# Hashed attention and a gated MLP on one core: totals moved behind the next product, a narrower shift product, and two groups of transposes moved to VectorE

## Chip, cores and metric

The kernel runs on one core of a Trainium2 chip. The time is the device time of one execution, in microseconds (us). Of the kernel before there are three timed runs and one profiled execution, whose rows are quoted further down. The engines are called TensorE (PE in the rows; PEld is its loading of weights), VectorE (DVE), ScalarE (ACT), GpSimd (POOL) and SyncE (SP, which issues most DMAs).

## What is computed

Four batches, 8 heads of 64 dimensions, 768 positions. Each position is hashed to a bucket by the signs of six projections; a query sees the keys of its own bucket. The attention output, heads side by side, is the input x of a gated MLP with residual.

```python
q_bucket = sum(((q @ proj) > 0) * powers);  k_bucket = sum(((k @ proj) > 0) * powers)
scores = where(q_bucket == k_bucket, q @ k.T / sqrt(D), -1e9)
attn = exp(scores - max(scores));  attn = attn / (sum(attn) + 1e-09);  x = attn @ v
h = gelu(x @ w_in);  u, v = split(h)                      # 512 and 512 columns
v_n = (v - mean(v)) / sqrt(var(v) + 1e-6) * g_ln
out = x + (u * (w_sg @ v_n + b_sg)) @ w_out
```

## The kernel before

**Attention.** Two heads make a pair, so there are 16 pairs, and each pair is done in two half pairs of 384 queries: 32 half pairs. `parts` and `features` turn q and k by transposes (L500), split them into a high and a low part and compute the sign features (L520). For each block of 128 queries `largest` computes scores in rows (L540) and VectorE takes their maxima (L545, two of 952 ns a block, three blocks a half pair). `shift` takes the smaller of the maxima into a mostly zero tile m of 128 columns for each block (L552, VectorE), and three matmuls with m as weights (L558) turn that into a row of the features, so that `weigh` computes scores that are already shifted (L578, four products for each key block), ScalarE takes the exponential into p (L582) and GpSimd adds the p tiles up (L595). `weighted` is the product with v (L606): p has a 385th column of ones, so that the same product also gives the plain sum over v, which a query without a key in its bucket needs.

`finish` closes a half pair: four matmuls of a 32-column matrix of ones with the sums (`total`, L621) give the totals, ScalarE adds 1e-9 (tile sm) and copies the product out (un, L626), the totals go through DRAM to get them on many partitions for the reciprocal and back as rs, and five operations then make xt = un * rs + e, where e is the correction for queries without keys (three on ScalarE, one on VectorE, one on GpSimd). xt goes to DRAM as xs, the MLP's x transposed.

**MLP.** It is done per batch. `load_x` loads x and splits it (xh by ScalarE, xl by GpSimd, L707). `hidden_v` (L774) and `hidden_u` (L805) are the two halves of the first product with the gelu behind them, `gate` (L823) multiplies with w_sg, `project` (L849) with w_out, with three matmuls for each product of split numbers. `gate_weights` (L733 to L742) is done once: it loads w_sg in rows, TensorE transposes 36 blocks, ScalarE copies the high parts and VectorE subtracts for the low parts wgl. `project` adds the residual on TensorE too: for each of its 24 tiles of 128 positions, four transposing matmuls of x (tile rx, L854) into the same PSUM bank, then ScalarE copies the bank into ob, and a DMA stores it.

**What sets the order.** Every step is added to a `Plan` with an engine, an assumed cost and a priority. `order()` is a list scheduler: it simulates the engines, the DMA queues and the eight PSUM banks and emits the steps in the order that comes out. The priorities are made from the table at the top (`MLP`, `HID`, `AVP`, `S0P`, `PREP`, `SHIFTP`, `FINP`, `WSTEP`, `WP`). What runs is the fixed order for each engine with semaphores between them. Six of the eight banks, in pairs, are used by the scores of both kinds, and any free one by the rest. `form` in the plan is the shape of the weights ("row": 64 rows by 128 columns, "col": 128 by 64, "col32": 128 by 32).

Of the kernel before, what the change touches and what calls it, by code (L numbers as in the profile page):

```python
# [21 lines left out]
MLP = {"xl": "POOL", "gm": "DVE", "gl": "POOL", "wg": 463.45, "wo": -43.61, "x": 464.83}  # L22

BANKED = False
HID = 277.32
AVP = 3.21
S0P = 0.22
AHEAD = 4
PREP, SHIFTP, FINP, WSTEP, WP = 4.15, -4.68, 2.34, 48.11, -68.38
# [4 lines left out]
class Plan:  # L34
# [76 lines left out]
    def order(self):  # L111
# [32 lines left out]
        while len(out) < len(G):  # L144
# [26 lines left out]
            if e == "PE":  # L171

                work = g["c"] + (self.TURN_PE[g["form"]] if g["form"] != form else 0.0)
                form = g["form"]
# [62 lines left out]
def kernel(  # L237
# [32 lines left out]
    SCALE = 1.0 / math.sqrt(D)  # L270
    MISS = 2.0 ** 33
# [19 lines left out]
    less = const.tile([P, 1], F32, name="less")  # L291
    nc.vector.memset(less, -1.0)
# [36 lines left out]

    msts = [const.tile([P, HT, P], F32R, name=f"m{i}") for i in range(2)]  # L330
# [57 lines left out]
    xs = [[dram.tile([P, S], F32, name=f"xs_{b}_{hp}") for hp in range(NP)] for b in range(B)]  # L388
# [49 lines left out]
    if True:  # L438
# [23 lines left out]
        for i, t in enumerate(ptiles):  # L462
            (nc.vector if i % 2 else nc.gpsimd).memset(t[:, :, SH:SH + 1], 1.0)
# [65 lines left out]
        def largest(st, t, prio):  # L529

            hf, i = divmod(t, HT)
            if i == 0:
                st.mx = late.ring([P, 2, HT, 2], F32, "mx", 3)
# [9 lines left out]
            for kh in range(2):  # L543
                plan.add(PE, 0.346, prio + 0.01 * kh, lambda kh=kh: mm(kh), [*st.hi, *st.ft], [sc[kh]], form="row")
                plan.add(DVE, 0.95, prio, lambda kh=kh: nc.vector.tensor_reduce(  # L545
                    mx()[:, kh, i, :], sc[kh]()[:, :, :SH], axis=AX.X, op=ALU.max, negate=True), [sc[kh]], [(mx, (kh, i))])

        def shift(st, hf, prio):

            mx, m, tp = st.mx, plan.buf("m", len(msts), lambda i: msts[i % len(msts)]), ps_one()  # L550
            V = nc.vector
            plan.add(DVE, 0.16, prio, lambda: V.scalar_tensor_tensor(  # L552
                m()[:, :, MROW::BL], mx()[:, 0], EMPTY, mx()[:, 1], op0=ALU.min, op1=ALU.min),
                     [mx], [m], port=True)
# [5 lines left out]
            plan.add(PE, 0.33, prio, spread, [m], [tp])  # L560
# [5 lines left out]
        def weigh(st, hf, k0, prio):  # L566

            cs, kts = slice(hf * SH, (hf + 1) * SH), (k0, k0 + 1)
            if k0 == 0:
                st.sum, st.p = held.ring([P, 2, SH], F32, "sum", 2), []  # L570
# [27 lines left out]
        def weighted(st, prio):  # L598

            st.av, p = ps_one(), st.p  # L600
            av = st.av

            def product():
                for kt in range(NT):
                    for j in range(2):
                        nc.tensor.matmul(av()[row(j), :SH + 1], st.v()[:, j, kt, :], p[kt]()[:, j, :], start=(kt == 0), stop=(kt == NT - 1))  # L606
# [311 lines left out]
```

## Time and profile before

| | us |
|---|---|
| median of three runs | 790.71 |
| lowest and highest | 790.60, 790.88 |
| span of the profiled execution | 791.5 |

The profiled execution is thus 0.8 us longer than the median. In it TensorE is busy for 767.8 us. The attention takes about the first 475 us, at some 13.7 us for each half pair; the four MLPs follow, with hidden_v of batch 0 and its hidden_u ahead of the transposed gate weights. A matmul group in a timeline row has its start, how long it lasts (neighbours overlap, since matmuls are pipelined, so that the distance between two starts is the time one takes), the line and the tiles; x4 at the end of a row counts instructions.

### The profile page before, as it was taken

The numbers are of one execution on the slowest core, as the hardware profiler recorded it, in microseconds if no ns is written. First come the engines' busy times: TensorE is split into PE (matmuls) and PEld (weight loads), VectorE is DVE, ScalarE is ACT, GpSimd is POOL, SyncE is SP. The second block draws the span as 40 slices with busy tenths as digits, with TensorE's granted clock in tenths as the row PEclk, the third lists the DMA queues.
The fourth block names the chain that finished last, engine by engine and source line by source line (L and its number), as shares of the span: only waits on it lengthen the run. The fifth ranks groups of instructions, "written<-read, shape, count | busy, mean of one in ns | idle before, by whom it ended". The sixth has DMA issues, their size and how long they took to land.

```text
span 791.5 us, 14719 instructions
## 1 busy us (share of the span) xinstructions
PE 767.8 (97%) x5480; PEld 613.0 (77%) x5480; DVE 536.9 (68%) x862; ACT 421.1 (53%) x742; POOL 481.0 (61%) x522
## 2 busy tenths in 40 slices
PE   4999999999999999999999999799999999999998
PEld 3777776767677676767767669798898889988996
DVE  7978888989889888666766437868932167407630
ACT  2366576666656665655655566625632266116511
POOL 1478889898878778776867774665742235404230
PEclk9899999999999999999999999999999999999999
DMA  7032443245334414321320123400115311040003
GB/s 204 23 77 69 110 116 99 70 112 124 74 97 94 104 47 91 92 70 53 82 58 25 32 54 138 144 28 28 43 64 160 100 60 41 1 150 12 1 0 133
DMA packets 99304, 60.91 MB, mean 77 GB/s; under 512 B 64288, under 2 KB 91040, under 8 KB 99232
## 3 DMA queue, kind: packets, MB, share of 16 engines
q1 hardware_dynamic: 97920, 56.94, 26.5%
q10 hardware_dynamic: 1312, 3.02, 1.2%
q8 instruction: 43, 0.70, 0.4%
q14 instruction: 29, 0.24, 0.1%
HBM read 47.16 MB, written 12.78 MB: 76 GB/s over the span
## 4 chain that ended last, share of the span: by engine, by line
PE 86%; DVE 8%; DMA 2%; ACT 1%; issue 1%; POOL 0%; DVEq 0%; ACTq 0%; POOLq 0%; SPq 0%
PE psb L578 16%; PE psb L606 16%; PE psb L823 13%; PE psb L540 10%; PE psb L849 8%; PE psb L774 6%; PE psb L805 5%; PE psb L520 5%; PE psb L500 2%; DVE mx L545 2%; PE psb L621 2%; PE psb L558 2%; PE psb L854 1%; DVE m L552 1%; DMA sq<-s 1%
## 5 line engine op out<-in xcount | busy, mean ns | idle before, releaser
L595 POOL TENSOR_TENSOR sum<-sum,p 128x384 f32<-128x384 f32 x256 | 243.6, 983 | 8.4 <-ACT p L582 8.4
L545 DVE TENSOR_REDUCE mx<-psb 128x2 f32<-128x768 f32 x192 | 174.7, 952 | 63.1 <-PE psb L540 61.8
L582 ACT ACTIVATE p<-psb 128x768 f32<-128x768 f32 x192 | 145.7, 812 | 61.6 <-PE psb L578 60.2
L606 PE MATMUL psb<-p,v 128*64 128x385 f32 x768 | 131.2, 491 | 0.0
L606 PEld LDWEIGHTS psb<-p,v 128*64 128x64 f32 x768 | 52.3, 137 | 64.0 <-issue 62.8
L595 POOL TENSOR_TENSOR sum<-p,p 128x384 f32<-128x384 f32 x64 | 64.2, 1026 | 60.9 <-ACT p L582 60.9
L540 PE MATMUL psb<-fk,fq 64*128 64x384 f32 x384 | 72.6, 372 | 2.8 <-DVE mx L545 1.7
L759 DVE SCALAR_TENSOR_TENSOR h<-h,psb 128x384 f32<-128x384 f32 (+1 forms) x56 | 32.8, 606 | 58.5 <-ACT h L758 58.5
L834 POOL TENSOR_TENSOR gs<-gt,gs 128x384 fp32r<-128x384 f32 x32 | 33.2, 1041 | 59.2 <-ACT gs L831 59.2
L578 PE MATMUL psb<-hq,hk 64*128 64x384 f32 x384 | 68.8, 352 | 0.0
L540 PE MATMUL psb<-hk,hq 64*128 64x384 f32 x384 | 65.5, 335 | 0.0
L849 PE MATMUL psb<-woh,gs 128*128 128x512 f32 x192 | 65.4, 402 | 0.0
L578 PE MATMUL psb<-fq,fk 64*128 64x384 f32 x384 | 65.1, 332 | 0.0
L578 PE MATMUL psb<-lq,hk 64*128 64x384 f32 x384 | 65.0, 332 | 0.0
L578 PE MATMUL psb<-hq,lk 64*128 64x384 f32 x384 | 64.9, 332 | 0.0
L823 PE MATMUL psb<-wgh,zh 128*128 128x384 f32 x192 | 64.3, 335 | 0.0
L823 PE MATMUL psb<-wgh,zl 128*128 128x384 f32 x192 | 64.2, 334 | 0.0
L823 PE MATMUL psb<-wgl,zh 128*128 128x384 f32 x192 | 64.2, 334 | 0.0
L540 PEld LDWEIGHTS psb<-fk,fq 64*128 64x128 f32 x384 | 36.6, 185 | 30.2 <-issue 13.0
L826 DVE TENSOR_TENSOR gt<-psb,b_bc 128x384 f32<-128x384 f32 x32 | 17.8, 556 | 58.4 <-PE psb L823 34.9
L784 POOL TENSOR_TENSOR mv<-mv,epsr 128x1 f32<-128x1 f32 x24 | 14.1, 588 | 67.8 <-DVE mv L783 67.7
L626 ACT COPY un<-psb 128x385 f32<-128x385 f32 x32 | 15.5, 483 | 68.2 <-PE psb L606 68.2
(127 smaller groups left out, 1751.8 us busy)
## 6 DMA issues: line engine op xcount, KB each, us to landing
q<-in_q_dram SPq DMA_DIRECT2D x32, 192.0 KB
k<-in_k_dram SPq DMA_DIRECT2D x32, 192.0 KB
v<-in_v_dram SPq DMA_DIRECT2D x16, 384.0 KB
rs<-r SPq DMA_DIRECT2D x64, 96.0 KB
xs<-xt SPq DMA_DIRECT2D x32, 192.0 KB
x<-xs SPq DMA_DIRECT2D x16, 384.0 KB
rx<-xs SPq DMA_DIRECT2D x96, 64.0 KB
out_dram<-ob SPq DMA_DIRECT2D x24, 256.0 KB
```

Of the source, the lines that this page charges most:

```text
L520: nc.tensor.matmul(fp()[:, hf, :SH], w[:, s, :], x()[:, hf * SH:(hf + 1) * SH], start=(i == 0), stop=(i == 2))
L540: nc.tensor.matmul(sc[kh]()[:, j, :SH], x[0]()[row(j), qs], x[1]()[row(j), kh * SH:(kh + 1) * SH], start=(n == 0), stop=(n == 1))
L545: plan.add(DVE, 0.95, prio, lambda kh=kh: nc.vector.tensor_reduce(mx()[:, kh, i, :], sc[kh]()[:, :, :SH], axis=AX.X, op=ALU.max, negate=Tr ...
L578: nc.tensor.matmul(sc[i]()[:, j, :SH], x()[row(j), ks], y()[row(j), cs], start=(n == 0), stop=(n == 3))
L582: plan.add(ACT, 0.81, prio, lambda i=i: nc.scalar.activation(p[i]()[:, :, :SH], sc[i]()[:, :, :SH], AF.Exp), [sc[i]], [p[i]])
L595: plan.add(POOL, 1.03, prio + 0.6, lambda i=i, j=j, first=first: nc.gpsimd.tensor_add(sums()[:, j], (first or sums)()[:, j, :SH], p[i]()[: ...
L606: nc.tensor.matmul(av()[row(j), :SH + 1], st.v()[:, j, kt, :], p[kt]()[:, j, :], start=(kt == 0), stop=(kt == NT - 1))
L774: nc.tensor.matmul(ps(), x()[:, ts_], w[:, c, FH:FF], start=(c == 0 and n == 0), stop=(c == NC - 1 and n == 2))
L805: nc.tensor.matmul(ps()[:, :SH], w[:, c, fs], x()[:, cs], start=(c == 0 and n == 0), stop=(c == NC - 1 and n == 2))
L823: nc.tensor.matmul(vp()[:, :SH], z()[:, t, fs], w()[:, t, cs], start=(t == 0 and n == 0), stop=(t == NT - 1 and n == 2))
L834: nc.gpsimd if e == POOL else nc.vector).tensor_sub(gl()[:, cs], gt(), gh()[:, cs].bitcast(F32)),
L849: nc.tensor.matmul(po(), a()[:, ts_], w()[:, f, :], start=(f == 0 and n == 0), stop=False)
```

## The change

In the attention, `weighted` now issues the totals of the half pair before right behind the product with v, in one step; `last` does them for the final half pair. The ring of sums has three tiles instead of two, un has four. The 385th column of p is 1e-9/768 instead of one, so that one VectorE operation makes xt = (un + un's last column) * rs; the three ScalarE steps on e and vm and GpSimd's addition are gone. `shift` uses 66 instead of 128 columns of m as weights, and its minimum is a reduction over three values, one of them a constant.

In the MLP, w_sg comes by 24 DMAs of 768-byte runs into 32 x 32 blocks that lie so that VectorE's transpose (it turns blocks of 32 x 32) gives the wanted tile; ScalarE copies and GpSimd subtracts in tiles of 768 columns. rx of `project` comes in four DMAs a tile with 128-byte runs, VectorE transposes it into ob and later adds the bank to it; the four transposing matmuls and ScalarE's copy are gone. For the loads to reach over four pairs at once xs is one DRAM tile for each batch, and an rx load waits for all four pairs of its batch. The numbers in the planner's table change: those for the gate's weights, the output's weights and the load of x in `MLP`, and most of the others.

```diff
-MLP = {"xl": "POOL", "gm": "DVE", "gl": "POOL", "wg": 463.45, "wo": -43.61, "x": 464.83}
+MLP = {"xl": "POOL", "gm": "DVE", "gl": "POOL", "wg": 471.24, "wo": 97.53, "x": 447.95}
+NSUM = 3
-AVP = 3.21
-S0P = 0.22
+AVP = 0.98
+S0P = 2.0
...
-            (nc.vector if i % 2 else nc.gpsimd).memset(t[:, :, SH:SH + 1], 1.0)
+            (nc.vector if i % 2 else nc.gpsimd).memset(t[:, :, SH:SH + 1], 1e-9 / S)
...
-            plan.add(DVE, 0.16, prio, lambda: V.scalar_tensor_tensor(
-                m()[:, :, MROW::BL], mx()[:, 0], EMPTY, mx()[:, 1], op0=ALU.min, op1=ALU.min),
+            W = BL + 2
+            plan.add(DVE, 0.16, prio, lambda: nc.vector.tensor_reduce(
+                m()[:, :, MROW::BL], mx(), axis=AX.X, op=ALU.min), [mx], [m])
...
-                    nc.tensor.matmul(tp()[:, i * P:(i + 1) * P], m()[:, i, :], identr, start=True, stop=True)
+                    nc.tensor.matmul(tp()[:W, i * P:(i + 1) * P], m()[:, i, :W], identr, start=True, stop=True)
...
+                def both():
+                    product()
+                    total(sums, tp)
+                plan.add(PE, 1.3 * HT + 0.5, prio, both, p + [v_, sums], [av, tp], form=("col", "col32"))
...
-            plan.add(PE, 0.375, prio, total, [sums], [tp], form="col32")
...
-            plan.add(DVE, 0.56, prio, lambda: V.tensor_mul(xt(), un()[:, :SH], rs()), [un, rs], [xt], port=True)
-            plan.add(POOL, 0.98, prio, lambda: nc.gpsimd.tensor_add(xt(), xt(), e()), [xt, e], [xt])
+            plan.add(DVE, 0.56, prio, lambda: V.scalar_tensor_tensor(
+                xt(), un()[:, :SH], un()[:, SH:SH + 1], rs(), op0=ALU.add, op1=ALU.mult), [un, rs], [xt], port=True)
...
-                        nc.tensor.transpose(tp()[:, i * P:(i + 1) * P], wv[:, hf * HT + i, :], ident)
...
-                plan.add(PE, 0.36, prio + t, tr, [w], [tp])
-                plan.add(ACT, 0.37, prio + t, high, [tp], [(wgh, (t, hf))])
-                plan.add(DVE, 0.47, prio + t, low, [tp, (wgh, (t, hf))], [(wgl, (t, hf))])
...
+            plan.add(DVE, 0.96, prio + t, tr, [w], [wt])
+            plan.add(ACT, 0.84, prio + t, lambda wt=wt, ts_=ts_: nc.scalar.copy(wgh()[:, :, ts_], six(wt)), [wt], [(wgh, t)])
+            plan.add(POOL, 1.88, prio + t, lambda wt=wt, ts_=ts_: nc.gpsimd.tensor_sub(
...
+                    xs[b][:, t * P + g * Q:t * P + (g + 1) * Q].rearrange("(f b) a -> b f a", b=Q)), xd[b], [(rx, g)])
+            plan.add(DVE, 0.7, p0 - 5, lambda rx=rx, ob=ob: nc.vector.transpose(ob(), rx()), [rx], [ob])
...
-            plan.add(PE, 0.43, p0 + 0.1, residual, [rx], [po])
-            plan.add(ACT, 0.59, p0, lambda ob=ob, po=po: nc.scalar.copy(ob(), po()), [po], [ob])
+            plan.add(DVE, 0.7, p0, lambda ob=ob, po=po: nc.vector.tensor_add(ob(), po(), ob()), [po, ob], [ob])
```

In the order of instructions the change shows at three places. The first is TensorE in the attention, at the totals of a half pair; sum is the tile that GpSimd adds up, the rows above and below it are scores in rows (fk, fq the features, hk, hq and lq, lk the high and low parts) and the product with v. Before:

```order
L540 MATMUL psb<-fk_1_857,fq_1_839 128x384 x2
L540 MATMUL psb<-hk_1_686,hq_1_664 128x384 x2
L621 MATMUL psb<-sum_926,ones 32x192 x4
L578 MATMUL psb<-hq_1_664,hk_1_686 128x384 x2
L578 MATMUL psb<-hq_1_664,lk_1_700 128x384 x2
L578 MATMUL psb<-lq_1_692,hk_1_686 128x384 x2
L578 MATMUL psb<-fq_1_839,fk_1_857 128x384 x2
```

The same place on TensorE after the change (L610 is the product, L632 the totals, L544 and L581 the two kinds of scores):

```order
L610 MATMUL psb<-p_153,v_247 64x385 x2
L610 MATMUL psb<-p_154,v_247 64x385 x2
L632 MATMUL psb<-sum_728,ones 32x192 x4
L544 MATMUL psb<-fk_1_813,fq_1_792 128x384 x2
L544 MATMUL psb<-hk_1_663,hq_1_630 128x384 x2
L581 MATMUL psb<-hq_1_630,hk_1_663 128x384 x2
L581 MATMUL psb<-hq_1_630,lk_1_668 128x384 x2
L581 MATMUL psb<-lq_1_656,hk_1_663 128x384 x2
L581 MATMUL psb<-fq_1_792,fk_1_813 128x384 x2
```

The totals have moved from among the scores to the end of the product, where the weights already have few columns; and one block's row scores (L544, four matmuls) now stand between the groups of eight of L581, where before two blocks' stood together.

The second place is TensorE in the project of the last batch, where one tile of 128 positions ends and the next begins (woh and wol are w_out, gs the gated values). Before:

```order
L849 MATMUL psb<-woh_6049,gs_8480 128x512
L849 MATMUL psb<-wol_6070,gs_8480 128x512
L849 MATMUL psb<-woh_6049,gs_8488 128x512
L854 MATMUL psb<-ident,rx_8567 128x128 x4
L849 MATMUL psb<-woh_6049,gs_8339 128x512
L849 MATMUL psb<-wol_6070,gs_8339 128x512
L849 MATMUL psb<-woh_6049,gs_8344 128x512
```

And the same place after:

```order
L863 MATMUL psb<-woh_5868,gs_8190 128x512
L863 MATMUL psb<-wol_5885,gs_8190 128x512
L863 MATMUL psb<-woh_5868,gs_8198 128x512
L863 MATMUL psb<-woh_5868,gs_8049 128x512
L863 MATMUL psb<-wol_5885,gs_8049 128x512
L863 MATMUL psb<-woh_5868,gs_8054 128x512
```

The transposing matmuls are gone and nothing stands in their place: one tile's products follow the other's.

The third place is TensorE behind hidden_u of batch 0 (xh and xl are the split x, wih and wil the first weights, the gs rows w_sg before its transposes). Before:

```order
L805 MATMUL psb<-xh_2181,wih 128x384
L805 MATMUL psb<-xl_2273,wih 128x384
L805 MATMUL psb<-xh_2181,wil 128x384
L733 MATMUL psb<-ident,gs_5714 128x128 x6
L733 MATMUL psb<-ident,gs_5718 128x128 x6
L733 MATMUL psb<-ident,gs_5726 128x128 x6
L733 MATMUL psb<-ident,gs_5732 128x128 x6
L733 MATMUL psb<-ident,gs_5747 128x128 x6
L733 MATMUL psb<-ident,gs_5763 128x128 x6
L774 MATMUL psb<-wih,xh_5957 128x512
L774 MATMUL psb<-wil,xh_5957 128x512
L774 MATMUL psb<-wih,xl_5967 128x512
```

And after (L816 is hidden_u, L785 hidden_v of the next batch):

```order
L816 MATMUL psb<-xh_2221,wih 128x384
L816 MATMUL psb<-xl_2340,wih 128x384
L816 MATMUL psb<-xh_2221,wil 128x384
L785 MATMUL psb<-wih,xh_5764 128x512
L785 MATMUL psb<-wil,xh_5764 128x512
L785 MATMUL psb<-wih,xl_5773 128x512
```

The 36 transposes are gone, and the next batch's hidden_v, which needs that batch's split x, follows directly. Over the whole stretch 57 matmuls of that hidden_v stand ahead of the gate of batch 0, where before there were 15.

## Rows read from the trace of the kernel before

**Rows 1.** The page: busy time of each engine; then the chain's shares by engine.

```profile
PE 767.8 (97%) x5480; PEld 613.0 (77%) x5480; DVE 536.9 (68%) x862; ACT 421.1 (53%) x742; POOL 481.0 (61%) x522
...
PE 86%; DVE 8%; DMA 2%; ACT 1%; issue 1%; POOL 0%; DVEq 0%; ACTq 0%; POOLq 0%; SPq 0%
```

**Rows 2.** Windows: stretch, us, PE, PEld, DVE, ACT, POOL busy, clock, DMA share, GB/s.

```profile
30.00:120.00 90.00, 90.00 (x791) 65.72 (x789) 77.60 (x103) 57.71 (x96) 74.04 (x78) 1.00 0.31 82
690.00:712.00 22.00, 22.00 (x111) 18.23 (x110) 1.12 (x2) 4.04 (x7) 1.55 (x2) 1.00 0.40 129
```

**Rows 3.** TensorE's timeline at one half pair's totals: start, duration, instructions.

```profile
94.48 0.44 PE L540 MATMUL psb<-fk,fq 64*128 64x384 f32 x2
94.76 0.34 PE L540 MATMUL psb<-hk,hq 64*128 64x384 f32 x2
94.93 0.34 PE L540 MATMUL psb<-fk,fq 64*128 64x384 f32 x2
...
97.12 0.45 PE L540 MATMUL psb<-fk,fq 64*128 64x384 f32 x2
97.41 0.34 PE L540 MATMUL psb<-hk,hq 64*128 64x384 f32 x2
97.67 0.53 PE L621 MATMUL psb<-sum,ones 128*32 128x192 f32 x8
98.14 0.45 PE L578 MATMUL psb<-hq,hk 64*128 64x384 f32 x2
98.42 0.34 PE L578 MATMUL psb<-hq,lk 64*128 64x384 f32 x2
```

**Rows 4.** The same view at the shift's product (L558).

```profile
88.59 0.34 PE L520 MATMUL psb<-lq,pwh 128*128 128x384 f32 x1
88.84 0.55 PE L558 MATMUL psb<-identr,m 128*128 128x128 f32 x3
89.23 0.40 PE L520 MATMUL psb<-hk,pwh 128*128 128x384 f32 x1
89.47 0.34 PE L520 MATMUL psb<-hk,pwl 128*128 128x384 f32 x1
```

**Rows 5.** Groups by shape: busy us, mean ns, idle before and what ended it.

```profile
L558 PEld LDWEIGHTS psb<-identr,m 128*128 128x128 f32 x96 | 13.5, 193 | 8.4 <-DVE m L552 7.2 <-ACT p L582 0.7 <-issue 0.3
L500 PEld LDWEIGHTS psb<-ident,q 128*128 128x128 f32 x96 | 10.7, 146 | 6.9 <-issue 4.2 <-DVE wy L374 2.7
L545 DVE TENSOR_REDUCE mx<-psb 128x2 f32<-128x768 f32 x192 | 174.7, 952 | 63.1 <-PE psb L540 61.8 <-ACT h L758 0.6
L826 DVE TENSOR_TENSOR gt<-psb,b_bc 128x384 f32<-128x384 f32 x32 | 17.8, 556 | 58.4 <-PE psb L823 34.9 <-POOL gs L834 23.5
L707 POOL TENSOR_TENSOR xl<-x,xh 128x768 fp32r<-128x768 f32 x16 | 29.8, 1870 | 3.2 <-ACT xh L709 3.2
```

**Rows 6.** The chain of waits in the last project: start, duration, engine and line.

```profile
768.59 2.77 PE psb L849 x12
771.35 0.44 PE psb L854 x4
771.79 2.78 PE psb L849 x12
```

**Rows 7.** TensorE's timeline around the gate's transposes; in brackets a wait and its releaser.

```profile
496.10 3.17 PE L733 MATMUL psb<-ident,gs 128*128 128x128 f32 x21
...
504.31 0.47 PE L774 MATMUL psb<-wih,xh 128*128 128x512 f32 x1
...
507.62 0.50 PE L774 MATMUL psb<-wih,xh 128*128 128x512 f32 x1 [1.67 <-DVE wgl L742]
...
509.82 0.34 PE L823 MATMUL psb<-wgh,zh 128*128 128x384 f32 x1
```

**Rows 8.** Windows: transfers in 256-byte pieces; hidden_u of batch 1. Columns as Rows 2.

```profile
380.00:386.00 6.00, 6.00 (x47) 3.45 (x46) 3.42 (x6) 2.98 (x8) 4.59 (x5) 1.00 0.89 178
540.00:570.00 30.00, 28.16 (x140) 26.24 (x139) 27.54 (x68) 18.54 (x38) 18.98 (x28) 0.94 0.08 23
```

More of the change, by code (lines that the diff above doesn't have):

```diff
@@ L328 @@
     nc.vector.memset(fv[:, 3, :, MROW:MROW + 1], 1.0)
+    mxs = [const.tile([P, HT, 2, 3], F32, name=f"mx{i}") for i in range(3)]
+    for t in mxs:
+        nc.vector.memset(t[:, :, :, 2:3], EMPTY)
     msts = [const.tile([P, HT, P], F32R, name=f"m{i}") for i in range(2)]
@@ L387 @@
     PE, DVE, ACT, POOL, SP = "PE", "DVE", "ACT", "POOL", "SP"
-    xs = [[dram.tile([P, S], F32, name=f"xs_{b}_{hp}") for hp in range(NP)] for b in range(B)]
+    xs = [dram.tile([DM, S], F32, name=f"xs_{b}") for b in range(B)]
     plan = Plan()
@@ L605, in product @@
                     for j in range(2):
[L606 to L613 removed]
+                        nc.tensor.matmul(av()[row(j), :SH + 1], v_()[:, j, kt, :], p[kt]()[:, j, :], start=(kt == 0), stop=(kt == NT - 1))
@@ new lines, in weighted @@
+            if owed is None:
+                plan.add(PE, 1.3 * HT, prio, product, p + [v_], [av], form="col")
+            else:
+                sums, tp = owed.sum, ps_one()
+                def both():
+                    product()
+                    total(sums, tp)
+                plan.add(PE, 1.3 * HT + 0.5, prio, both, p + [v_, sums], [av, tp], form=("col", "col32"))
+            half.un = un = late.ring([P, SH + 1], F32, "un", 4)
+            plan.add(ACT, 0.48, prio - 1, lambda: nc.scalar.copy(un(), av()[:, :SH + 1]), [av], [un])
@@ new lines, in weighted, with total, last @@
+            if owed is not None:
+                finish(owed, tp, prio)
+            return half
+        def total(sums, tp):
+            for j in range(2):
+                for a in range(2):
+                    r = 64 * j + 32 * a
+                    nc.tensor.matmul(tp()[r:r + 32, :QH2], ones, sums()[:, j, a * QH2:(a + 1) * QH2], start=True, stop=True)
+        def last(half, prio):
+            sums, tp = half.sum, ps_one()
+            plan.add(PE, 0.375, prio, lambda: total(sums, tp), [sums], [tp], form="col32")
+            finish(half, tp, prio)
@@ L614, in finish @@
+        def finish(st, tp, prio):
+            hf, un = st.hf, st.un
+            sm = late.ring([P, QH2], F32, "sm", 3)
             sq, rs, xt = late.ring([P, W6], F32, "sq", 3), late.ring([P, SH], F32, "rs", 3), late.ring([P, SH], F32, "xt", 2)
             V = nc.vector
-            def total():
-                for j in range(2):
-                    for a in range(2):
-                        r = 64 * j + 32 * a
-                        nc.tensor.matmul(tp()[r:r + 32, :QH2], ones, sums()[:, j, a * QH2:(a + 1) * QH2], start=True, stop=True)
@@ L680 @@
                 if c % HT == HT - 1:
[L681 to L682 removed]
+                    owed = weighted(sts[n], hf, 2 * g + AVP, owed)
+        last(owed, 2 * g + FINP)
     M_ = MLP
```

86 lines of the change are left out of this document (34 added, 52 removed).

## The prediction

> **What bounds the kernel now.** The page comes first: TensorE is busy for 767.8 of 791.5 us, and 86% of the chain of waits is TensorE's [rows 1]. The windows tell where that is a hard bound. In 90 us of the attention and in 22 us of the last project TensorE is busy without a gap at a granted clock of 1.00, which is the 2.4 GHz level [rows 2]. There a us taken from TensorE is a us of the end, until another engine is full. VectorE is the nearest: 77.60 of 90 us, 11.8 us of a half pair of 13.7; GpSimd has 74.04. In the project VectorE has 1.12 of 22 us. So prices are read as distances between starts in TensorE's timeline, and each one asks whether VectorE or GpSimd can follow.
>
> **Totals.** Two plain pairs of score matmuls start 0.17 us apart (94.76 to 94.93) [rows 3]. Around the totals the distances are 0.26 (97.41 to 97.67), 0.47 (to 98.14) and 0.28 (to 98.42), in all 1.01 us for three steps of which two are plain pairs, 0.34. The totals cost 0.67, of which about 0.20 is the change into another shape of weights and back. Behind the product the weights already have few columns, and the change back to the scores is paid by the product anyway, as at 94.48 to 94.76 (0.28). What remains is the 0.47 of the totals themselves, or 0.36 if the 0.11 that a first pair pays goes as well. So 0.20 to 0.31 is saved, 31 times (the last total stands alone): 6.2 to 9.6 us. I take **6.2**, since going from 64 to 32 columns is a change of shape too, and every change in the rows costs something. If it costs 0.10 more than that, 3.1 stay. The sums are those of the half pair before, finished some 13 us earlier, so the product waits for nothing new. Three ScalarE operations and GpSimd's 0.98 us go from each half pair; neither engine bounds here, so I count nothing for them. The one VectorE operation that replaces a multiplication of the same tile is also counted at nothing; if it went at half speed, VectorE would have 0.56 us more in 13.7, which its idle 1.9 hide.
>
> **Spread.** From 88.59 to 89.47 TensorE takes 0.88 us for three matmuls with m and two plain ones [rows 4]. The part from 88.84 to 89.23 is 0.39; less the 0.11 of a first pair, 0.28 remain, 0.093 for each. The columns that move through (128) don't change, only those of the weights, 128 to 66. If the weights' load sets the step, 62/128 of 0.28 goes, 0.13 a half pair, 4.2 us for 32; from the whole 0.39 it would be 0.19, 6.0 us. If the moving columns set it, nothing. I take **4.2**, because the load of these weights takes 193 ns [rows 5], longer than the step, so that it can't be hidden by one neighbour. A loss is bounded by the difference of two loads of 128 columns, 193 against 146 ns: 0.05 a half pair, -1.6 us.
>
> These loads are of fp32r; loads of 128 fp32 columns (L500) take 146 ns, less than the 193, so no row shows the fp32r load as the fast one [rows 5]. The Trainium skill, "TensorE: Matmul & The Clock Gate", section "Weight-path perf modes — Fast Weight Load (FWL) and DoubleRow", says that a fast load is on when there are exactly 128 weights and the type isn't FP32, measured at about twice the speed; 66 columns would then lose it. The rival for it is below.
>
> **Residual on VectorE.** In the last project a tile with its four transposing matmuls takes 3.20 us (768.59 to 771.79), of which 0.44 lie between 771.35 and 771.79 [rows 6]. 24 tiles: **10.6** us. The cover must hold: VectorE gets a transpose and an addition of 512 columns in each tile. An addition from PSUM of 384 columns takes 556 ns [rows 5], so 741 ns for 512, 1.5 us for both, in 2.77 us of TensorE and on an engine that is nearly idle there. A 32 x 32 transpose isn't in the trace; at twice an addition both take 2.2, still covered. The loads: a tile is 262 KB, before in pieces of 512 bytes, now of 128. A window with 256-byte pieces moves 178 GB/s at a share of 0.89, so 200 at full share [rows 8]. Half the piece at half the rate is an estimate of 100 GB/s, 2.6 us for a tile. That is close to 2.77, but the gate's 144 matmuls stand ahead of the project: two tiles can be loaded and turned into ob, and two more loaded, before the project starts, and only two of six remain. SP issues as many DMAs as before. If the cover fails, the rival on loads has the price.
>
> **Gate weights on VectorE.** The block of transposes lasts from 496.10 to 504.31, 8.2 us, and at 507.62 TensorE waits another 1.67 us for the last low part before the gate can start at 509.82 [rows 7]. Both go: 9.9 us. But the block also covered the split of the next batch's x. Its tiles are free only when the last hidden_u of batch 0 is through, and now the next hidden_v stands right there. The first low part needs 1.87 us on GpSimd [rows 5] behind ScalarE's copy, so at least 2 us are exposed; with all four parts one after the other 7.5 us. The new order takes one part of x with several tiles of positions in a row, which hides the later parts; I take 3.4 exposed, **6.5** net, and keep 2 to 8 (10 if the split is done ahead).
>
> **What the new numbers of the planner do.** Two places. In the row scores, one step goes from 97.12 to 97.41, 0.29 where a plain one takes 0.17, with the longer first row of an engine that had stopped [rows 3]. Here TensorE had caught up with the engines that empty the banks. One or two such stops in each half pair are 3.8 to 7.7 us in all. In the new order four matmuls of row scores alternate with eight of the shifted ones, so the two engines that empty banks take turns; half of the stops should go: **3**, with 6 either way, since the new alternation can stop elsewhere. And in hidden_u of batch 1, from 540 to 570, TensorE is busy for 28.16 of 30 us at a mean clock of 0.94 [rows 8]: 1.8 us idle and 1.8 by the clock, which falls behind a stop. The new order may heal it or make another: **0**, 4 either way.
>
> **Sum.** 6.2 + 4.2 + 10.6 + 6.5 + 3 + 0 = 30.5 us of 791.5: a span of 761.0. The profiled execution was 0.8 longer than the median of the runs, which gives **760** us.
>
> **Rivals.**
> - *The narrow weights and the order bring nothing* (moving columns set the step, the stops stay): 760 + 4.2 + 3 = 767. For it: the number of columns that move is unchanged, and which engine stops TensorE isn't settled. Against it: the 193 ns.
> - *The fast load is lost* with 66 columns. At half the speed a load of 66 columns lasts 193 x 2 x 66/128 = 199 ns, as long as before: the 4.2 go, 764. Against it stand the 146 ns of a type that would never be fast.
> - *GpSimd makes the MLP wait.* It now has the low parts of the gate weights (six of about 1.87 us, 11.2) beside those of x (7.5), 18.7 us together. If they come one after the other behind hidden_u, the 57 matmuls of hidden_v that stand ahead of the gate, 13 us at the 0.23 that one of 512 columns takes [rows 6], don't cover them: 5.6 us of wait, and the 6.5 of the gate weights are lost: 772. Against it: w_sg doesn't depend on x and can be done during hidden_u.
> - *Loads set the project.* A tile would have to take 10 us (26 GB/s): the fifth, whose load can start some 6 us in, when its buffer is free, would land at 16 and the sixth at 26, where TensorE ends at 16.6, so 9.4 us at the end of the last batch; in the other batches TensorE goes on: 769. Against it: 100 GB/s is what the rows make likely. The Trainium skill, "DMA: Bandwidth & Descriptors", section "Specifications", puts the smallest transfer for full rate at 512 bytes, so 128-byte runs are below it; by that rule alone the loads get slower, as in the estimate, and only the size of it decides.
> - *The alternation makes VectorE the bound of the row scores, slower than before.* Four row matmuls and eight shifted ones last 2 x 0.17 + 4 x 0.17 = 1.04 us, and VectorE's maximum for them 0.952 [rows 5]. Only 0.09 is left for its other work in that stretch. If each of six alternations in a half pair came 0.17 late, 192 x 0.17 = 33 us would be lost, 793; that is the point from which the change is slower. For it: VectorE has 11.8 - 6 x 0.95 = 6.1 us of other work in each half pair. Against it: that work can lie beside the product (4 us) and the features, and 14% of VectorE's time is idle.
> - *Nothing changes*, since what TensorE no longer does was a wait for others: 790. The windows without a gap speak against it.
>
> **Chances.** My forecast 0.60, narrow weights and order without effect 0.18, fast load lost 0.04, GpSimd 0.08, loads 0.04, VectorE bound 0.04, nothing 0.02. The range is **750 to 772**: the terms' own bounds go to 3.1, -1.6, 2, -3 and -4 on the bad side and 9.6, 6.0, 8, 9 and 4 on the good side; they won't all fall on one side, and some 10 to 12 us either way remain. Faster by over 0.2% (about what a measurement of this kernel can tell from no change): 0.94; within 0.2%: 0.02; slower: 0.04.
>
> **What would show it.** Right: in the trace of after the product is followed by the totals 0.4 to 0.5 us before the next scores, with no totals among the scores; the shift's three matmuls take some 0.26 instead of 0.39; the tiles of the projects follow each other at 2.77 us; hidden_v of batch 1 starts within 2 to 4 us behind hidden_u of batch 0; VectorE's idle time in the attention is above 10%. Wrong: TensorE's rows of scores with waits on VectorE's maxima in each alternation; a wait ahead of the gate on GpSimd's low parts; project tiles that wait for ob or for rx; a half pair that isn't at 13.3 us, which is 13.7 less 0.20, 0.13 and 0.1.

## The result

The kernel after takes 758.14 us (median of four runs, 757.51 to 758.49), before on the same chip 790.8. The ratio is 0.9574 with a 95% interval of 0.9558 to 0.959: 4.3% faster, some 33 us. The forecast was 760, in a range of 750 to 772. The time agrees; the terms of the sum don't all agree, and the errors cancel. That is what the experiments are about. Their effects are given as differences of such ratios times 790.8, since each group of runs had its own runs of the kernel before beside it.

The page of the kernel after, busy times and the chain by engine, to be held against [rows 1]:

```profile
PE 731.8 (97%) x5348; PEld 594.0 (79%) x5348; DVE 563.8 (75%) x906; ACT 376.0 (50%) x616; POOL 464.4 (61%) x496
...
PE 84%; DVE 7%; DMA 6%; issue 1%; ACT 1%; SPq 0%; ACTq 0%; DVEq 0%
```

TensorE has 36.0 us less work and is still busy for 97%: it still bounds the kernel. Windows of the kernel after (columns as [rows 2]): the attention, and the stretch behind hidden_u of batch 0:

```profile
30.00:120.00 90.00, 89.17 (x807) 66.49 (x805) 78.53 (x104) 53.10 (x82) 72.94 (x75) 1.00 0.34 84
...
475.00:490.00 15.00, 11.58 (x32) 7.99 (x33) 12.50 (x19) 8.92 (x16) 10.84 (x10) 0.66 0.82 157
```

The attention runs at full clock with VectorE idle for 13%, and one half pair follows the other at 13.13 us instead of 13.78 (mean distance between the starts of two products with v). The second row is new: TensorE busy for 11.58 of 15 us at a mean clock of 0.66.

Where the time went is read best by adding, for each line, the distances from each matmul's start to the next one's start, over the whole trace. A wait thus counts for the line that ran before it. A second trace of the kernel before (the run before_again below) serves as the base, since it is the more ordinary one:

| TensorE's time, start to start, us | before | after | difference |
|---|---|---|---|
| scores, both kinds (L540 + L578; L544 + L581) | 223.9 | 213.5 | -10.4 |
| totals (L621; L632) | 14.8 | 14.8 | 0.0 |
| shift's product (L558; L561) | 13.0 | 8.3 | -4.8 |
| turning q and k, features (L500 + L520; L504 + L524) | 70.4 | 63.8 | -6.6 |
| project and residual (L849 + L854; L863) | 76.8 | 66.8 | -10.0 |
| gate's transposes (L733) | 8.1 | none | -8.1 |
| hidden_v (L774; L785) | 71.4 | 77.2 | +5.8 |
| hidden_u (L805; L816) | 69.6 | 71.1 | +1.5 |
| product with v, gate, start | 234.1 | 234.4 | +0.3 |
| sum | 782.1 | 749.8 | -32.3 |

### The profile page after: what moved, and what is told of

It reads as the page before. It is cut to its first block, busy times and chain, and to the rows that moved or that the text cites. A ratio compares the mean times of both kernels' runs of the same rounds, so it can differ in the third digit from the quotient of the medians.

```text
span 755.7 us, 14344 instructions
## 1 busy us (share of the span) xinstructions
PE 731.8 (97%) x5348; PEld 594.0 (79%) x5348; DVE 563.8 (75%) x906; ACT 376.0 (50%) x616; POOL 464.4 (61%) x496
## 4 chain that ended last, share of the span: by engine, by line
PE 84%; DVE 7%; DMA 6%; issue 1%; ACT 1%; SPq 0%; ACTq 0%; DVEq 0%
PE psb L581 17%; PE psb L610 15%; PE psb L834 11%; PE psb L863 9%; PE psb L544 9%; PE psb L785 7%; PE psb L816 7%; PE psb L524 4%; PE psb L504 3%; PE psb L632 2%; DMA x<-xs 2%; DMA gs<-in_moe_w_sg_dram 1%; DMA ow<-in_moe_w_out_dram 1%; DVE mx L549 1%; PE psb L561 1%
## 5 line engine op out<-in xcount | busy, mean ns | idle before, releaser
L598 POOL TENSOR_TENSOR sum<-sum,p 128x384 f32<-128x384 f32 x256 | 247.8, 1004 | 0.0
L549 DVE TENSOR_REDUCE mx<-psb 128x2 f32<-128x768 f32 x192 | 181.5, 956 | 50.2 <-PE psb L544 41.8
L585 ACT ACTIVATE p<-psb 128x768 f32<-128x768 f32 x192 | 155.5, 815 | 62.0 <-PE psb L581 58.4
L610 PE MATMUL psb<-p,v 128*64 128x385 f32 x768 | 131.2, 491 | 0.0
L610 PEld LDWEIGHTS psb<-p,v 128*64 128x64 f32 x768 | 52.3, 137 | 63.2 <-issue 60.8
L544 PE MATMUL psb<-fk,fq 64*128 64x384 f32 x384 | 68.3, 352 | 2.2 <-DVE fk L527 1.2
L581 PE MATMUL psb<-hq,hk 64*128 64x384 f32 x384 | 65.4, 337 | 2.0 <-DVE mx L549 1.2
L581 PE MATMUL psb<-fq,fk 64*128 64x384 f32 x384 | 64.4, 332 | 0.0
L544 PE MATMUL psb<-hk,hq 64*128 64x384 f32 x384 | 64.4, 332 | 0.0
L581 PE MATMUL psb<-lq,hk 64*128 64x384 f32 x384 | 64.3, 331 | 0.0
L581 PE MATMUL psb<-hq,lk 64*128 64x384 f32 x384 | 64.3, 331 | 0.0
L863 PE MATMUL psb<-woh,gs 128*128 128x512 f32 x192 | 60.4, 391 | 0.8 <-DVE ob L866 0.8
L769 ACT ACTIVATE h<-psb 128x384 f32<-128x384 f32 (+1 forms) x56 | 29.6, 535 | 55.7 <-PE psb L785 42.0
L801 POOL TENSOR_TENSOR zl<-y,zh 128x512 fp32r<-128x512 f32 x24 | 32.7, 1361 | 29.6 <-ACT zh L800 29.5
L544 PEld LDWEIGHTS psb<-fk,fq 64*128 64x128 f32 x384 | 35.9, 184 | 13.4 <-issue 6.4
```

Of the source, the lines that this page charges most:

```text
L544: nc.tensor.matmul(sc[kh]()[:, j, :SH], x[0]()[row(j), qs], x[1]()[row(j), kh * SH:(kh + 1) * SH], start=(n == 0), stop=(n == 1))
L581: nc.tensor.matmul(sc[i]()[:, j, :SH], x()[row(j), ks], y()[row(j), cs], start=(n == 0), stop=(n == 3))
L585: plan.add(ACT, 0.81, prio, lambda i=i: nc.scalar.activation(p[i]()[:, :, :SH], sc[i]()[:, :, :SH], AF.Exp), [sc[i]], [p[i]])
L598: plan.add(POOL, 1.03, prio + 0.6, lambda i=i, j=j, first=first: nc.gpsimd.tensor_add(sums()[:, j], (first or sums)()[:, j, :SH], p[i]()[: ...
L610: nc.tensor.matmul(av()[row(j), :SH + 1], v_()[:, j, kt, :], p[kt]()[:, j, :], start=(kt == 0), stop=(kt == NT - 1))
L863: nc.tensor.matmul(po(), a()[:, ts_], w()[:, f, :], start=(f == 0 and n == 0), stop=(f == NF - 1 and n == 2))
```

## The experiments

**Totals apart.** The totals are a step of their own again, among the scores.

```diff
-                    owed = weighted(sts[n], hf, 2 * g + AVP, owed)
-        last(owed, 2 * g + FINP)
+                    last(weighted(sts[n], hf, 2 * g + AVP, None), 2 * g + 2.34)
```

> The kernel after, with the totals of each half pair as a step of their own among the score matmuls, not behind the product; three of the four planner costs and all else stay. Theory (each change of the weights' shape costs TensorE about 0.1 us on the way in and out): +0.20 us a half pair, +6.2 us for 31, so about 764. Rival (the place of the totals is worth nothing, what was gained is GpSimd's and ScalarE's lighter work and the order of the scores): 758, as the kernel after.

Measured: 771.87 us, ratio 0.9742 (0.9723 to 0.9761), +13.3 us against the kernel after, twice the theory's number. TensorE's timeline of this run at one of the totals, start and duration first:

```profile
91.90 0.34 PE L581 MATMUL psb<-fq,fk 64*128 64x384 f32 x2
92.71 0.53 PE L632 MATMUL psb<-sum,ones 128*32 128x192 f32 x8 [0.47 <-DVE mx L549]
93.17 0.44 PE L544 MATMUL psb<-fk,fq 64*128 64x384 f32 x2
93.45 0.34 PE L544 MATMUL psb<-hk,hq 64*128 64x384 f32 x2
```

The steps are 0.81, 0.46 and 0.28 us. The usual distance into the totals is 0.27 (median of the 32 half pairs; the 0.81 here has a wait in it), and 0.27 + 0.28 less two plain 0.17 is 0.20: the price of the two changes of shape, as forecast. In the same sums as above (the profiled execution of this run took 773.37) the scores take 9.6 us more, the two hidden products 5.8. So 6.2 is the shape, and the rest is stops and a different order in the MLP, which this edit moves as well. The rival, that the place is worth nothing, is out.

**Width of the shift's product.**

```diff
-            W = BL + 2
+            W = P
```

> The kernel after, with 128 instead of 66 weight columns in the shift's product and nothing else changed, the order of all instructions included. Theory (the load of the weights sets the step; in the traces 0.112 us a matmul at 128 columns and 0.060 at 66): 3 x 0.052 x 32 = +5.0 us, about 763. Rival 1 (the moving columns set it, and what shrank around this product was a wait for VectorE): 758. Rival 2 (a fast load that only 128 columns get): faster than the kernel after, below 758.

Measured: 762.79 us, ratio 0.9626 (0.9608 to 0.9644), +4.1 us. TensorE's timeline at this product, first with 66 columns (kernel after), then with 128 (this run):

```profile
108.93 0.34 PE L524 MATMUL psb<-lq,pwh 128*128 128x384 f32 x1
109.11 0.34 PE L561 MATMUL psb<-identr,m 128*66 128x128 f32 x3
109.29 0.39 PE L524 MATMUL psb<-hk,pwh 128*128 128x384 f32 x1
```

```profile
110.07 0.34 PE L524 MATMUL psb<-lq,pwh 128*128 128x384 f32 x1
110.25 0.45 PE L561 MATMUL psb<-identr,m 128*128 128x128 f32 x3
110.53 0.39 PE L524 MATMUL psb<-hk,pwh 128*128 128x384 f32 x1
```

Three matmuls take 0.18 us against 0.28, and their weights' load 137 ns (mean after) against 193 [rows 5]. The number of weight columns sets the step, as the columns that move through are the same. The rival with moving columns is out, and so is the one with a fast load for 128 columns: 66 are faster by more than a third, with no sign that 128 had an advantage to lose.

**Residual on TensorE.**

```diff
-            plan.add(DVE, 0.7, p0 - 5, lambda rx=rx, ob=ob: nc.vector.transpose(ob(), rx()), [rx], [ob])
-            plan.add(DVE, 0.7, p0, lambda ob=ob, po=po: nc.vector.tensor_add(ob(), po(), ob()), [po, ob], [ob])
+            plan.add(PE, 0.43, p0 + 0.1, residual, [rx], [po])
+            plan.add(ACT, 0.59, p0, lambda ob=ob, po=po: nc.scalar.copy(ob(), po()), [po], [ob])
```

> The kernel after, with the residual added on TensorE as before (four transposing matmuls a tile, ScalarE's copy), loads of rx in 512-byte runs. Theory (TensorE bounds the projects): +0.42 us a tile, +10 us for 24, about 768. Rival (VectorE's additions and the 128-byte loads cost part of it back): +5 or less, 763.

Measured: 770.9 us, ratio 0.9727 (0.9713 to 0.9742), +12.1 us. The chain of the last project in this run has the same two rows as [rows 6], at the same durations:

```profile
746.14 2.77 PE psb L860 x12
748.91 0.44 PE psb L865 x4
749.35 2.78 PE psb L860 x12
```

Ten to eleven of the twelve us are these matmuls, the rest is order in the MLP. Nothing of the gain was given back on VectorE or by the loads. In the kernel after, the groups of VectorE's transposes and additions (busy, mean ns, idle before) are these:

```profile
L859 DVE STREAM_TRANSPOSE ob<-rx 128x512 f32<-128x512 f32 x24 | 16.8, 704 | 5.7 <-DMA out_dram<-ob 4.5 <-DVE y L797 0.8 <-DMA rx<-xs 0.3
L866 DVE TENSOR_TENSOR ob<-psb,ob 128x512 f32<-128x512 f32 x24 | 16.3, 685 | 19.4 <-PE psb L863 19.1
```

Both were estimated at 741 ns. The 128-byte loads are waited for 0.3 us in all, and TensorE's project waits once for ob, 0.8 us.

**Gate weights on TensorE.** The loop of the kernel before is put back whole; its core:

```diff
-            plan.add(DVE, 0.96, prio + t, tr, [w], [wt])
+                plan.add(PE, 0.36, prio + t, tr, [w], [tp])
```

> The kernel after, with the gate weights transposed on TensorE as before (36 transposes, 12 ScalarE copies, 12 VectorE subtractions). The prediction had 6.5 us for this edit. Theory after seeing the trace (VectorE is full from 455 to 490 us, its transposes of 1.65 us delay the gelu, and TensorE then waits 4.8 us behind hidden_u and runs at the low clock for some us): only about 3 us, so 761. Rival 1 (the prediction's step): 764 to 765. Rival 2 (it was a loss, the waits cost more than the transposes did): 756.

Measured: 756.42 us, ratio 0.9545 (0.953 to 0.956), 2.3 us *faster* than the kernel after; the two intervals just touch. The part of the change that was to bring 6.5 us brings nothing, and probably costs some 2. TensorE's timeline behind hidden_u, first of the kernel after, then of this run:

```profile
473.26 0.34 PE L816 MATMUL psb<-xh,wil 128*128 128x384 f32 x1
475.71 0.59 PE L785 MATMUL psb<-wih,xh 128*128 128x512 f32 x1 [2.11 <-ACT xh L726]
476.11 0.63 PE L785 MATMUL psb<-wil,xh 128*128 128x512 f32 x1
477.62 0.80 PE L785 MATMUL psb<-wih,xl 128*128 128x512 f32 x1 [0.88 <-POOL xl L724]
478.21 0.63 PE L785 MATMUL psb<-wih,xh 128*128 128x512 f32 x1
```

```profile
473.97 2.15 PE L750 MATMUL psb<-ident,gs 128*128 128x128 f32 x15
...
482.99 0.78 PE L791 MATMUL psb<-wih,xh 128*128 128x512 f32 x1
483.56 0.63 PE L791 MATMUL psb<-wil,xh 128*128 128x512 f32 x1
```

With the transposes on TensorE, the split x is there when they end, and hidden_v doesn't wait for it. (There are waits inside that block, 1.8 us for VectorE's gelu and 0.6 for a low part, and the granted clock is 0.66 from 480 to 485; the block takes 9.0 us.) Without the transposes TensorE waits for x, and the rows behind are 0.43 apart instead of 0.23: the clock has fallen to the low one of its two levels, 1.2 GHz (the granted clock is 0.50 from 480 to 485). At 481.51 there is a third wait, 1.82 us, for VectorE's gelu (u). The 57 matmuls up to the gate take 20.1 us where 13.2 are plain, and 2.3 are lost ahead of the first: 9.2 in all.

**Why VectorE's transposes bring nothing.** Two causes were looked for: VectorE itself, which is busy for 19.28 of the 20 us from 455 to 475 and needs 1.65 us for a transpose where the planner has 0.96, or the split of x. Three runs bear on it; they don't separate the two cleanly.

True cost: the planner is told 1.65, and four of its numbers are set anew for that.

```diff
-MLP = {"xl": "POOL", "gm": "DVE", "gl": "POOL", "wg": 471.24, "wo": 97.53, "x": 447.95}
+MLP = {"xl": "POOL", "gm": "DVE", "gl": "POOL", "wg": 392.54, "wo": -73.13, "x": 549.11}
-HID = 293.06
+HID = 297.72
-            plan.add(DVE, 0.96, prio + t, tr, [w], [wt])
+            plan.add(DVE, 1.65, prio + t, tr, [w], [wt])
```

> The kernel after, with the planner told what VectorE's transpose of a gate tile took in the trace, 1.65 us instead of 0.96, and four of its numbers (wg, wo, x, HID) set anew for that; the operations are the same. Theory (the transposes themselves are affordable, the loss against TensorE's transposes comes from placing them in a stretch where VectorE is full): 2 to 4 us faster than the kernel after, 754 to 756, and less wait of TensorE behind hidden_u of batch 0. Rival (VectorE has 9.9 us more to do between the attention and the first gate and any place costs the same): within 1 us of the kernel after.

Measured: 760.71 us, ratio 0.9598 (0.9581 to 0.9616), 1.9 slower. This placement is no better than the old one; others were not tried. Its trace shows VectorE in the way: in its order the gelu stands behind a transpose, the transpose waits for the load of its tile of w_sg, and TensorE waits 6.55 us behind hidden_u.

```profile
478.56 1.56 DVE L748 STREAM_TRANSPOSE gs<-gs 128x768 f32<-128x768 f32 x1 [3.47 <-DMA gs<-in_moe_w_sg_dram]
482.59 0.80 PE L785 MATMUL psb<-wih,xh 128*128 128x512 f32 x1 [6.55 <-DVE u L774]
```

Gate copy: a plain copy in place of each transpose, the order unchanged. It leaves out the transposing of the gate's weights.

```diff
-                nc.vector.transpose(wt().rearrange("p (s f b) -> p s f b", s=NT, b=Q),
-                                    w().rearrange("p (f a s) -> p s f a", f=P // Q, s=NT))
+                nc.vector.tensor_copy(wt(), w())
```

> The kernel after with the order unchanged, and a plain VectorE copy of 768 columns in place of the transpose of each gate tile, which leaves out the transposing of the gate's weights: about 0.9 instead of 1.65 us, six times, so 4.3 us less for VectorE between 457 and 489 us. Theory (VectorE is full there and TensorE waits for it): 2 to 4 us faster than the kernel after, 754 to 756. Rival (TensorE waits there for the split of the next batch's x, and VectorE's time is hidden): within 1 us.

Measured: 760.2 us, ratio 0.9593 (0.957 to 0.9616); against the kernel after +1.5, within the intervals. This doesn't clear VectorE, because the work was not taken from it: the six copies take 6.0 us in all instead of 9.8, but three other operations of VectorE take 3.5 more (the two of y in this stretch 2.33 and 2.31 us instead of 1.58 and 0.77, one of xt 1.80 instead of 0.64), and its busy time from 455 to 475 falls by 1.4 us only. The second y runs beside two subtractions of GpSimd and ends just behind them; ScalarE, in its order, waits for it ahead of the high part of x, and TensorE waits for x 4.60 us instead of 2.11:

```profile
471.34 3.96 POOL L755 TENSOR_TENSOR wgl<-gs,wgh 128x768 fp32r<-128x768 f32 x2
473.53 2.31 DVE L796 SCALAR_TENSOR_TENSOR y<-y,mv,g_bc 128x512 f32<-128x512 f32 x1
475.93 0.72 ACT L798 ACTIVATE y<-y,mv 128x512 f32<-128x512 f32 x1 [2.74 <-DVE y L796]
479.18 0.80 PE L784 MATMUL psb<-wih,xh 128*128 128x512 f32 x1 [4.60 <-ACT xh L726]
```

Batch 0's x in batch 1, which leaves out the load and the split of batch 1's x:

```diff
-        if b + 1 < B:
+        if 1 <= b and b + 1 < B:
             xx = load_x(b + 1, p + M_["x"])
```

> The kernel after, with the split x of batch 0 used for batch 1 too, which leaves out the load and split of batch 1's x. Theory (behind hidden_u of batch 0 TensorE waits 2.1 us for the high and 0.9 us for the low part of that x, and its clock is at the low level for some us after): 4 to 7 us faster than the kernel after, 751 to 754. Rival (VectorE's full stretch would make TensorE wait at the same place for the gelu instead): within 2 us.

Measured: 754.35 us, ratio 0.9521 (0.9502 to 0.954), 4.2 us faster. So the load and split of x are worth some 4 us here. They are not all of it: hidden_v and hidden_u take 148.2 us in the kernel after, 143.8 in this run and 138.2 in gate_pe, by the sums used above. (ScalarE and GpSimd are spared the work of that split too, and the order moves a little: 60 matmuls of hidden_v stand ahead of the gate.) The window of that stretch in this run has a mean clock of 0.89, against 0.66 in the kernel after, and TensorE still waits for VectorE's gelu in it:

```profile
475.00:490.00 15.00, 12.66 (x49) 9.82 (x48) 14.27 (x23) 8.74 (x18) 8.42 (x9) 0.89 0.71 126
...
482.95 0.50 PE L785 MATMUL psb<-wih,xh 128*128 128x512 f32 x1 [2.34 <-DVE u L774]
```

In the kernel after the split also comes later than it could, since ScalarE takes its work in order. In its timeline the high part of x (L726) starts 1.57 us behind the start of hidden_u's last matmul, with the gate's weights (L755), work on the last hidden_v tile and parts of the gelu ahead of it. Ahead of that work ScalarE had been idle for 1.48 us, waiting for an operation of VectorE that stood behind a transpose:

```profile
468.62 1.65 DVE L748 STREAM_TRANSPOSE gs<-gs 128x768 f32<-128x768 f32 x1
470.17 0.54 DVE L770 SCALAR_TENSOR_TENSOR h<-h,psb 128x384 f32<-128x384 f32 x1
470.74 0.52 ACT L772 ACTIVATE h<-h 128x384 f32<-128x384 f32 x1 [1.48 <-DVE h L770]
...
471.65 0.83 ACT L755 CAST wgh<-gs 128x768 fp32r<-128x768 f32 x1
472.46 0.73 ACT L799 ACTIVATE y<-y,mv 128x512 f32<-128x512 f32 x1
473.22 0.62 ACT L800 CAST zh<-y 128x512 fp32r<-128x512 f32 x1
...
474.83 0.83 ACT L726 CAST xh<-x 128x768 fp32r<-128x768 f32 x1 [0.19 <-issue]
```

The chain of waits of the kernel after, in this stretch, doesn't go over the split of x. It goes from a load of w_sg, which ScalarE issues in its order at 473.61, to the transpose (gs) and the gelu (u) behind it on VectorE, and from there to hidden_v:

```profile
474.10 3.70 DMA gs<-in_moe_w_sg_dram
477.80 1.70 issue
479.50 1.53 DVE gs L748
481.02 0.45 DVE u L774
...
481.51 14.46 PE psb L785 x51
```

So two things hold TensorE here: the split of x, worth some 4 us by a run, and VectorE's gelu, which stands behind transposes that wait for the loads of w_sg. The second is read from the traces; no run has these loads earlier or the transposes behind the gelu, so how the rest divides between the loads, VectorE's time and the clock is open.

**Gate weights on TensorE, with new numbers.** As gate_pe, with wg 193.19, wo 75.84, x 109.06 and HID 315.08.

```diff
-MLP = {"xl": "POOL", "gm": "DVE", "gl": "POOL", "wg": 471.24, "wo": 97.53, "x": 447.95}
+MLP = {"xl": "POOL", "gm": "DVE", "gl": "POOL", "wg": 193.19, "wo": 75.84, "x": 109.06}
```

> The kernel after with the gate weights transposed on TensorE as before, and the same four numbers of the planner set anew for that. Expected from both theories: at or somewhat below the 756.4 of the run with TensorE's transposes and unchanged numbers, 754 to 757. If VectorE's transposes, placed well, are as good, the run with the true cost reaches this one.

Measured: 757.32 us, ratio 0.9559 (0.9545 to 0.9573), no better than gate_pe. The best kernel measured that leaves nothing out is gate_pe, at 0.9545.

**The planner's numbers.** The kernel after with all of the numbers of before:

```diff
-S0P = 2.0
+S0P = 0.22
...
-PREP, SHIFTP, FINP, WSTEP, WP = 3.93, -4.13, 7.98, 30.06, -23.48
+PREP, SHIFTP, FINP, WSTEP, WP = 4.15, -4.68, 2.34, 48.11, -68.38
```

> The kernel after with the planner's numbers of before (the MLP table, HID, AVP, S0P and the five behind them); no operation differs, only their order. In the order of instructions one block's row scores then stand alone between the shifted scores 90 times instead of 181. Theory (the alternation lets VectorE empty the banks in time, which takes the stops of 0.1 to 0.2 us out of the row scores, 5 to 7 us in the traces; the rest of the numbers is placement in the MLP): +6 to +12 us, 764 to 770. Rival (the stops went because ScalarE, VectorE and GpSimd have less to do in each half pair, whatever the order): within 2 us of the kernel after.

Measured: 777.88 us, ratio 0.9819 (0.9803 to 0.9835), +19.4 us, more than the 12 that the theory had at most; the rival is out. By the start-to-start sums the scores take 12.5 us more and hidden_u 13.2, and hidden_v takes 5.6 less. Then a single number:

```diff
-S0P = 2.0
+S0P = 0.22
```

> The kernel after with one number of the planner set back: S0P, the due time of the row scores, 0.22 instead of 2.0. The alternation of row scores and shifted scores falls from 181 to 91 places. Theory (with two blocks of row scores in a row TensorE's weight load waits about 0.27 us for ScalarE's exponential to free a bank, twice in most half pairs, as in the trace of before): +9 to +13 us, 767 to 771, and these waits are back in the view of TensorE's weight loads. Rival (the 19 us by which the old numbers were slower came from the MLP's numbers): within 2 us of the kernel after.

Measured: 765.85 us, ratio 0.9662 (0.9641 to 0.9683), +7.0 us, somewhat less than the theory had and far from the rival's 2. By the start-to-start sums the row scores alone take 7.0 more. These waits are not seen in TensorE's busy share, since its matmul rows overlap; they are seen in the distances of starts and at the weight loads. Waits of the weight loads from 30 to 430 us (engine, line, waited for, us in total, times, longest), of before, of after and of this run:

```profile
PEld psb L540 <- ACT p L582: 7.5, 29, 0.3
PEld psb L558 <- DVE m L552: 6.5, 18, 0.6
```

```profile
PEld psb L581 <- DVE mx L549: 2.2, 3, 1.5
PEld psb L581 <- ACT p L585: 1.7, 3, 0.6
```

```profile
PEld psb L544 <- ACT p L585: 11.0, 39, 0.4
```

In before the second four matmuls of a block's row scores (four are half a block: one half of the keys) wait 29 times for ScalarE's exponential to free a bank. With the alternation no such wait is left in this stretch, and setting the one number back brings it back, with all the lighter work of the other engines in place. It comes back 39 times, more often than in the kernel before. And the number in the kernel before:

```diff
-S0P = 0.22
+S0P = 2.0
```

> The kernel before with this one number of the kernel after, S0P = 2.0. Theory (the alternation only fits because the totals no longer stand among the scores, where they hold TensorE in its order; without that the later due time makes the row scores late and VectorE the one that is waited for): slower than before, by 5 us or more, above 796. Rival (the number alone brings the gain, with no operation changed): 8 us or more faster than before, below 783.

Measured: 833.09 us, ratio 1.0516 (1.049 to 1.0542), 41 us slower than before. The waits of its weight loads, same stretch:

```profile
PEld psb L578 <- DVE mx L545: 15.2, 49, 0.6
PEld psb L578 <- ACT p L582: 11.4, 21, 2.1
```

VectorE's maxima are waited for 49 times, ScalarE's exponential 21 times. The direction is the theory's, its reason is not: in totals_apart the totals stand among the scores too, with S0P = 2.0, and it costs 13 us, not 41. What else lets the kernel after alternate was not tried by itself. Its VectorE has less to do in each half pair (the operation on xt takes 717 ns instead of 974, that on m 173 instead of 766), and its ScalarE three operations less.

**A second trace of before.**

> The kernel before, unchanged, for a second trace. The prediction took the span of the profiled execution, 791.5, to be 0.8 us above the median of the device times. Theory (a device time lies about 1.9 us above the span of the same execution, as for the kernel after, 757.5 against 755.7, and the profiled execution of before was a long one): a span near 789 and a device time near 791. Rival (span and device time agree for this kernel): a span near 791 for a device time of 791.

Measured: a span of 788.1 and a device time of 789.91. A device time lies 1.8 us above its span, here as in the kernel after (755.7 and 757.51).

## Why the prediction was right, and where only its sum was

- **What bounds it**: right. TensorE's time went down by 32.3 us start to start and the median by 32.7.
- **Totals**, 6.2 forecast: right. In the kernel after the totals are followed by the next scores 0.46 us later, they cost the same 14.8 us, and both changes of shape among the scores, 0.20 us in a half pair, are gone. The Trainium skill, "TensorEngine Tiling (Array Packing)", section "Key Properties", says that a change of the tiling mode drains TensorE; the trace agrees in that each of these two changes costs about 0.1 us.
- **Spread**, 4.2 forecast: right, 4.1 by the run with 128 columns. Three matmuls take 0.18 us, less than the 0.26 that was named as the mark.
- **Residual**, 10.6 forecast: right, 10.0 start to start and 12.1 by its run. The loads had the cover that was claimed for them.
- **Gate weights**, 6.5 forecast: wrong. The step that failed is "I take 3.4 exposed", a number between 2 and 7.5 that no row gave. For the waits on x it was close: 2.11 and 0.88 us, and hidden_v started 2.45 us behind the last matmul of hidden_u, inside the 2 to 4 that were named as a sign of being right. But 9.2 us were lost up to the gate. Two things had no price: VectorE's gelu, which came late behind transposes (1.82 us of wait), and the clock, which was low behind the waits and slowed the matmuls there from 0.23 to 0.43 us. hidden_v and hidden_u took 7.3 us more together and ate nearly all of the 8.1 that went.
- **Order of the scores**, 3 forecast: about right. The scores lost 10.4 us in the table; less the 6.2 of the totals, 4.2 are the order's. The 7.0 us of S0P are more, because the new code with the old number stops more often than the old code did (39 waits against 29). The row that was read ([rows 3], 97.12 to 97.41) shows only the second half of a stop, 0.12 us; the step before it loses 0.11 as well. Steps from one row score to the next lose 7.0 us less than before, and those from a row score to a shifted one 2.8 more, in six stops: the alternation stops elsewhere, as the term allowed.
- **A term that was missing.** Turning q and k and the features (L500, L520) lost 6.6 us, and no term stood for it. Its place is `shift`, whose minimum was read as the same work in another form. The groups of VectorE for it, before and after:

```profile
L552 DVE SCALAR_TENSOR_TENSOR m<-mx 128x6 fp32r<-128x6 f32 x32 | 24.5, 766 | 1.1
```

```profile
L556 DVE TENSOR_REDUCE m<-mx 128x6 fp32r<-128x18 f32 x32 | 5.5, 173 | 1.1
```

Six values a partition took 766 ns on average with two inputs from SBUF, and 173 as a reduction. The operation itself was not slower: the first one, with no GpSimd operation beside it, took 0.17 us, and all but one of the others ended within 0.04 us of the end of a GpSimd addition, most of them after some 0.88 us.

```profile
24.68 0.17 DVE L552 SCALAR_TENSOR_TENSOR m<-mx 128x6 fp32r<-128x6 f32 x1
87.91 0.88 DVE L552 SCALAR_TENSOR_TENSOR m<-mx 128x6 fp32r<-128x6 f32 x1
```

The product L558 stood behind it in TensorE's order: the 6.5 us of waits on m above are gone. [rows 5] had it in L558's own row, "DVE m L552 7.2", unread. The Trainium skill, "SBUF — State Buffer", section "Who interferes with whom", says that an operation of VectorE with two inputs in SBUF contends with a GpSimd operation that reads there, and that a reduction never does on trn2; these rows agree with it. No run has the reduction alone, so that the 6.6 us are its work is not shown. For it: 4.1 of them lie in the steps directly ahead of the shift's product, and old_numbers, which has the reduction with the planner's numbers of before, takes 66.3 us for these lines, some 4 less than the kernel before.
- **The conversion at the end** was a slip without effect. 791.5 was a span and 790.71 a device time; by the second trace a device time is 1.8 above the span, so the profiled execution was some 2.6 us longer than the median, not 0.8. Since the sum of 30.5 was in effect taken from the median, the result stands.
- **Sum.** By the table, against 30.5: totals and score order together gave 1.2 more, the spread 0.6 more, the residual 0.6 less, the lines without a term 6.6 more, the gate weights with both hidden products 5.7 less (0.8 of 6.5), the rest 0.3 less. That makes 32.3. That the time came out within 2 us of the forecast is in part luck: two errors of some 6 us, one each way, cancel.
- **A half pair** takes 13.13 us where the prediction named any other than 13.3 as a sign of being wrong. The sign was right to show: 0.65 us less in each half pair instead of 0.43, some 7 us in 32, is nearly the size of the term that was missing.
- **Rivals.** Narrow weights without effect and the fast load are out by spread_128, the loads by the 0.3 us of waits. GpSimd's wait ahead of the gate didn't come; its 0.88 us behind hidden_u did. VectorE as the bound of alternating scores is no idle threat: the kernel before with the same number waits for its maxima, and for ScalarE's exponential too, at 833.

## What to carry to other kernels

Before counting a transpose or a copy on the bound engine as waste, ask what is being made ready under it: here 8 us of transposes covered waits and a fall of the clock of nearly the same size. Ask also what stands behind the work in the order of the engine that takes it over: here the gelu stood behind transposes, and those waited for loads. Stops of a pipelined engine are to be looked for in the waits of its weight loads and in the distances of starts, since its busy share stayed at 97 to 100% over them. And the numbers of a scheduler belong to one code: S0P = 2.0 is worth 7 us in the new kernel and costs 41 in the old one.

## What was not expected of the hardware

A minimum of two inputs with six results a partition took 172 ns alone and some 880 beside GpSimd's additions; as a reduction over 18 values it took 164 to 175 beside them. VectorE's transpose of 32 x 32 blocks took 1.37 ns a column where it read in order (704 ns for 512) and 2.1 where it read with a stride of six values (1633 ns for 768). Six copies in place of transposes, 3.8 us shorter together, made other operations of VectorE 3.5 us longer, and the time didn't fall.
